# Cutting the token parts of a feed-forward stage as 384, 512, 512, 384 instead of 512, 512, 512, 256, with the weights split in the first two parts

## The chip, the core and the metric

The kernel runs on one core of one Trainium2 chip. The metric is the device time of one execution in microseconds (us); lower is better. The engines named below are PE (TensorE), DVE (VectorE), ACT (ScalarE), POOL (GpSimd) and SP (SyncE, which here issues the DMAs of the last stage).

## What is computed

Three layers follow each other: a sigmoid attention, a layer of eight experts of which one is taken per token, and a dense feed-forward layer with a rational activation. The change lies in the last one. For 1792 tokens of 768 values and a hidden width of 2048:

```python
h = x @ w_in
h2 = h * h
h3 = h2 * h
P = a[0] + a[1] * h + a[2] * h2 + a[3] * h3
Q = 1.0 + np.abs(b[0]) * np.abs(h) + np.abs(b[1]) * h2
g = P / (Q + 1e-06)
return (g @ w_out).astype(np.float32)
```

## The kernel before

`attention` and `experts` run first and are not touched. While they run, they also decode the weights of the last layer to single precision and leave them in DRAM (`wd`), 16 blocks of 128 hidden columns, each holding its slice of `w_in` and of `w_out`.

`ffn` (lines 849 to 1029) is the last stage. The tokens are cut into parts (`Q`, line 855): 512, 512, 512 and 256. Within a part it runs over the 16 blocks (`f`); one block of one part is called a unit here, and `i` counts the 64 units. To keep single precision, every operand is split in a high half and a low half that TensorE takes in its faster format, and every product is made of three matmuls (high by high, low by high, high by low).

A unit has these steps:

- `l1(i)`: 18 matmuls (lines 941, 942 and 945), input `xh`, `xl` by the unit's `w_in` block, into one PSUM bank `ph`. There are two such banks.
- `act1` and `act2`: the activation on the bank, five ACT instructions and eight DVE instructions (lines 953 to 976). The last two leave the halves `gh` and `gl`.
- `l2(i)`: 18 matmuls (lines 989 to 991), `gh`, `gl` by the unit's `w_out` block, added into six PSUM banks `acc` that hold the part's output. At the last block of a part these are copied out (`ot`, lines 995 and 997) and stored (line 998).

Each engine takes its instructions in program order. The loop (lines 1011 to 1029) sets that order: in turn `i` PE gets `l1(i)` and then `l2(i - 2)`, so two units of lead lie between a unit's first and second product, and the activation runs in them.

In the first part (`i < 16`) the weights come raw: `load` (line 866) fetches a block from `wd`, `split` (line 881) makes the halves of it by two ACT copies and two DVE subtractions of 128x768 (lines 888, 889), two units ahead, and `keep` (line 891) stores the halves to `ws`. In the later parts `fetch` (line 875) reads the halves back. SP issues all of these in program order.

The next part's tokens are prepared meanwhile: at `f == 2` they are loaded (`rows`, line 896), at `f` 5 to 8 DVE multiplies one chunk of 128 tokens a unit by its gate (`gate`, line 905, instruction at line 910), and at `f` 9 to 14 `xprep` (line 912) makes one of six blocks of `xh` and `xl` a unit: PE transposes (line 918) into a `ph` bank, an ACT copy (line 919), a DVE subtraction (line 920). The first part's tokens are prepared by `first_x` (line 922), after 26 matmuls on constants (line 927) that keep PE at work while the tokens are fetched.

The order of DVE's work in a turn is: the gate or the `xl` subtraction of that turn, the two subtractions of `split(i + 2)`, and the eight instructions of the activation.

Of the kernel before, what the change touches and what calls it, by code (L numbers as in the profile page):

```python
# [8 lines left out]
F32 = mybir.dt.float32  # L9
F32R = mybir.dt.float32r  # L10
# [10 lines left out]
P = 128  # L21
B, H, S, D = 4, 12, 448, 64
NT = B * S
# [4 lines left out]
KD = DM // P  # L28
# [15 lines left out]
def build(tc, qT, kT, v, emb, tau, w1, w2, w_in, w_out, pa, pb, out, dbg=None):  # L44
    nc = tc.nc
    with ExitStack() as ctx:
        ctx.enter_context(tc.manual_schedule())
        cst = ctx.enter_context(tc.tile_pool(name="cst", bufs=1))
        drm = ctx.enter_context(tc.tile_pool(name="drm", bufs=1, space=DRAM))
        st = dict(cst=cst, drm=drm, dbg=dbg, nc=nc, w1=w1, w2=w2, raw={})  # L50
        stg = ctx.enter_context(tc.tile_pool(name="stg", bufs=5))
        st["stg"] = stg
        st["wd"] = drm.tile([F2 // P, P, 2, DM], F32, name="wd")
        st["ws"] = [drm.tile([F2 // P, P, 2, DM], F32, name=f"ws{i}") for i in range(2)]
        st["rdy"] = [tc.alloc_semaphore(f"rdy{i}") for i in range(4)]
        with tc.tile_pool(name="wq", bufs=1) as wq:
            st["W"] = [[wq.tile([P, KD, 512], F32R, name=f"w{u}{x}") for x in "hl"] for u in range(2)]
            attention(tc, st, qT, kT, v, emb, tau, w_in, w_out, pa, pb)
            experts(tc, st, w1, w2, w_in, w_out)
        ffn(tc, st, out)  # L60
        if dbg is not None:
            dump(tc, st, dbg)
# [786 lines left out]
def ffn(tc, st, out):  # L849
    nc = tc.nc  # L850
    wd, yd, ident = st["wd"], st["yd"], st["ident"]
    gt = st["gr"]
    co, ab1, one = st["co"], st["ab1"], st["one"]
    NF = F2 // P
    Q = [(t, min(512, NT - t)) for t in range(0, NT, 512)]
    NQ = len(Q)
    NU = NQ * NF
    LF = 2
    with ExitStack() as ctx:
        fw = ctx.enter_context(tc.tile_pool(name="fw", bufs=2, reuse_waits="tile"))  # L860
# [3 lines left out]
        X, R, WI, WO, G, acc, KEPT = {}, {}, {}, {}, {}, {}, {}  # L864

        def load(i):
            if i < NF:
                R[i] = st["stg"].tile([P, 2, DM], F32, name="rw", tag="raw")
                nc.sync.dma_start(R[i], wd[i])

        def pair(i):
            for part, D_, n in ((0, WI, 4), (1, WO, 6)):
                D_[i] = fw.tile([P, 2, DM], F32R, name="wi" if part == 0 else "wo", bufs=n)

        def fetch(i):
            if NF <= i < NU and i not in WI:
                pair(i)
                for part, D_ in ((0, WI), (1, WO)):
                    nc.sync.dma_start(D_[i].bitcast(F32), st["ws"][part][i % NF])

        def split(i):
            if i >= NF:
                return
            raw = R.pop(i)
            pair(i)
            for part, D_ in ((0, WI), (1, WO)):
                w = KEPT[part, i] = D_[i]
                nc.scalar.copy(w[:, 0], raw[:, part])
                nc.vector.tensor_sub(w[:, 1], raw[:, part], w[:, 0])

        def keep(i):
            if 0 <= i < NF:
                for part, D_ in ((0, WI), (1, WO)):
                    nc.sync.dma_start(st["ws"][part][i], KEPT.pop((part, i)).bitcast(F32))

        def rows(q, parts):
            t0, w = Q[q]
            yq = fp.tile([P, 4, DM], F32, name="yq", bufs=1)
            src = yd[t0 : t0 + w].rearrange("(c p) d -> p c d", p=P)
            n = w // P // parts  # L900
            for c in range(0, w // P, n):
                nc.sync.dma_start(yq[:, c : c + n], src[:, c : c + n])
            X[q] = dict(y=yq, n=w, c=w // P)

        def gate(q, c):
            if c >= X[q]["c"]:
                return
            ci = Q[q][0] // P + c
            y = X[q]["y"][:, c]
# [11 lines left out]

        def first_x():
            d = X[0]
            d["h"], d["l"] = [fw.tile([P, KD, 512], F32R, name=n) for n in ("xh", "xl")]
            pts = [ppa.tile([P, 512], F32, name=f"acc{k}") for k in range(KD)]
            for _ in range(26):
                nc.tensor.matmul(pts[0], lhsT=st["ones"], rhs=st["wz"], start=True, stop=True)  # L927
            for c in range(4):
                for k in range(KD):
                    nc.tensor.transpose(pts[k][:, c * P : (c + 1) * P], d["y"][:, c, k * P : (k + 1) * P], ident)  # L930
            for k in range(KD):
                nc.scalar.copy(d["h"][:, k], pts[k])  # L932
                nc.vector.tensor_sub(d["l"][:, k], pts[k], d["h"][:, k])

        def l1(i):
            w = WI.pop(i)
# [30 lines left out]
        def act2(i, t1, q, r0):  # L967
            w = Q[i // NF][1]
            n = fp.tile([P, 512], F32, name="n")[:, :w]
            nc.vector.scalar_tensor_tensor(n, q, 1.000001, r0, op0=ALU.add, op1=ALU.mult)  # L970
            nc.vector.scalar_tensor_tensor(n, n, 2.0, r0, op0=ALU.subtract, op1=ALU.mult, reverse0=True)  # L971
            nc.vector.scalar_tensor_tensor(t1, t1, co[:, 0:1], n, op0=ALU.add, op1=ALU.mult)  # L972
            gh = fp.tile([P, 512], F32R, name="gh", bufs=3)[:, :w]
            gl = fp.tile([P, 512], F32R, name="gl", bufs=3)[:, :w]
            nc.vector.tensor_copy(gh, t1)  # L975
            nc.vector.tensor_sub(gl, t1, gh)  # L976
            G[i] = (gh, gl)

        def l2(i):
            q, f = divmod(i, NF)  # L980
            w = WO.pop(i)
            t0, m = Q[q]
            gh, gl = G.pop(i)
# [16 lines left out]
        for i in range(4):  # L1000
            load(i)
        split(0)
        split(1)
        rows(0, 4)
        keep(0)
        load(4)
        load(5)
        for c in range(4):
            gate(0, c)
        first_x()  # L1010
        for i in range(NU + LF):
            if i < NU:
                q, f = divmod(i, NF)
                if q + 1 < NQ:
                    if f == 2:
                        rows(q + 1, 1)
                    if 5 <= f < 9:
                        gate(q + 1, f - 5)
                    if 9 <= f < 9 + KD:
                        xprep(q + 1, f - 9)  # L1020
                ph = l1(i)
                split(i + 2)
                keep(i + 1)
                load(i + 6)
                fetch(i + 2)
                fetch(i + 3)
                act2(i, *act1(ph, X[i // NF]["n"]))
            if i >= LF:
                l2(i - LF)
# [44 lines left out]
```

## Time and profile before

| what | value |
|---|---|
| median of 3 runs | 1059.98 us (1059.35 to 1060.36) |
| the profiled execution | 1062.73 us, span 1061.0 us from its first to its last instruction |
| PE busy | 1015.2 us, 96% of the span |
| PE weight loads busy | 798.5 us, 75% |
| DVE busy | 720.4 us, 68% |
| ACT busy | 516.4 us, 49% |
| mean granted TensorE clock | 0.983 of full speed |
| last stage | first product at 587.43 us, last matmul at 1056.72 us |

The shares are means over the whole program. The last stage takes some 470 us of it, and within it the first part has other work on DVE, ACT and the DMA queues than the rest, so the shares have to be read part by part.

### The profile page before, as it was taken

To read this page: it belongs to the slowest core of one execution; us is meant where nothing else is said; L and a number is where in the kernel's file an instruction comes from. 1 tells how busy PE (TensorE), PEld (TensorE's weight loads), DVE (VectorE), ACT (ScalarE), POOL (GpSimd) and SP (SyncE) were. 2 spreads that over 40 slices of the span, in tenths; PEclk is the share of its full clock that TensorE was granted. 3 is DMA by queue.
4 is the path that set the end of the run, shared out by engine and by line. 5 is a ranking of instruction groups with operands and counts; after the bars stand their busy time and mean duration, and the time that the engine had idled before them with its cause. 6 is when DMAs were issued, how large, how long until landed. Compare 5 with 4: busy or idle time off the path is not lost. (4 is left out here: it accounts for less than half of the span.)

```text
span 1061.0 us, 14341 instructions
## 1 busy us (share of the span) xinstructions
PE 1015.2 (96%) x5227; PEld 798.5 (75%) x5228; DVE 720.4 (68%) x1036; ACT 516.4 (49%) x871; POOL 133.0 (13%) x141
## 2 busy tenths in 40 slices
PE   8999999487999999999996999999999999999998
PEld 3444444276898989889884788888888888888998
DVE  2567667579901988083955899976677666666686
ACT  5565656442323323233333676745555455554664
POOL 2000000024322332242433000000000000000000
PEclk9999999789999999999998999999999999999999
DMA  7999987578731887275767997586755566555892
GB/s 232 264 273 290 300 261 222 182 264 282 251 128 62 269 268 253 105 227 184 230 182 217 415 365 289 223 299 235 272 185 180 187 237 240 198 181 193 316 407 93
DMA packets 105580, 250.99 MB, mean 237 GB/s; under 512 B 11785, under 2 KB 59081, under 8 KB 105489
## 3 DMA queue, kind: packets, MB, share of 16 engines
q1 hardware_dynamic: 102416, 235.19, 65.9%
q0 software_dynamic: 3072, 14.58, 4.0%
q8 instruction: 58, 0.95, 0.4%
q14 instruction: 34, 0.27, 0.1%
HBM read 194.68 MB, written 55.06 MB: 235 GB/s over the span
## 5 line engine op out<-in xcount | busy, mean ns | idle before, releaser
L989 PE MATMUL acc<-gh,wo 128*128 128x512 f32 (+1 forms) x384 | 139.3, 363 | 0.3 <-DVE gh L975 0.3
L991 PE MATMUL acc<-gl,wo 128*128 128x512 f32 (+1 forms) x384 | 139.4, 363 | 0.0
L990 PE MATMUL acc<-gh,wo 128*128 128x512 f32 (+1 forms) x384 | 139.2, 363 | 0.0
L941 PE MATMUL ph<-xh,wi 128*128 128x512 f32 (+1 forms) x384 | 137.8, 368 | 0.1
L942 PE MATMUL ph<-xh,wi 128*128 128x512 f32 (+1 forms) x384 | 136.1, 363 | 0.0
L953 ACT COPY h<-ph 128x512 f32<-128x512 f32 (+1 forms) x64 | 34.0, 532 | 158.1 <-PE ph L945 158.1
L960 DVE SCALAR_TENSOR_TENSOR sq<-sq,ab,ab 128x512 f32<-128x512 f32 (+1 forms) x64 | 43.8, 684 | 91.8 <-ACT ab L957 91.8
L176 ACT ACTIVATE A<-sc,bias_s 128x896 f32<-128x896 f32 x96 | 88.7, 1008 | 27.2 <-PE sc L173 25.3
L616 DVE CAST w0h<-raw 128x1536 fp32r<-128x1536 f32 x14 | 12.8, 957 | 115.9 <-ACTq L741 115.0
L945 PE MATMUL ph<-xl,wi 128*128 128x512 f32 (+1 forms) x384 | 87.2, 363 | 0.0
L941 PEld LDWEIGHTS ph<-xh,wi 128*128 128x128 f32 x384 | 72.5, 189 | 12.1 <-ACT xh L932 1.3
L989 PEld LDWEIGHTS acc<-gh,wo 128*128 128x128 f32 x384 | 72.5, 189 | 11.7 <-DVE gh L975 0.6
L991 PEld LDWEIGHTS acc<-gl,wo 128*128 128x128 f32 x384 | 72.5, 189 | 11.5 <-DVE gl L976 0.2
L990 PEld LDWEIGHTS acc<-gh,wo 128*128 128x128 f32 x384 | 72.5, 189 | 11.2
L942 PEld LDWEIGHTS ph<-xh,wi 128*128 128x128 f32 x384 | 72.5, 189 | 10.8
L173 PE MATMUL sc<-qr,kr 64*128 64x448 f32 x384 | 78.7, 549 | 0.0
L185 PE MATMUL po<-A,vt 128*64 128x448 f32 x384 | 77.5, 545 | 0.0
L945 PEld LDWEIGHTS ph<-xl,wi 128*128 128x128 f32 x384 | 66.7, 189 | 11.2
L728 PE MATMUL py<-w2h,h 128*128 128x384 f32 x256 | 62.8, 344 | 4.9 <-DVEq L625 4.0
L728 PE MATMUL ph<-w0h,x 128*128 128x512 f32 x192 | 59.6, 410 | 8.3 <-DVEq L625 3.7
L738 ACT ACTIVATE hs<-ph 128x512 f32<-128x512 f32 x38 | 22.7, 598 | 81.8 <-PE ph L728 81.8
L728 PE MATMUL py<-w3h,h 128*128 128x384 f32 x256 | 61.3, 339 | 0.0
(199 smaller groups left out, 1975.7 us busy)
## 6 DMA issues: line engine op xcount, KB each, us to landing
raw<-in_w_dram SPq DMA_DIRECT2D x64, 768.0 KB, 6.8
wi<-ws SPq DMA_DIRECT2D x48, 768.0 KB, 4.3
wo<-ws SPq DMA_DIRECT2D x48, 768.0 KB, 4.4
raw<-in_w_in_dram SPq DMA_DIRECT2D x16, 768.0 KB, 6.9
raw<-in_w_out_dram SPq DMA_DIRECT2D x16, 768.0 KB, 7.2
wd<-dec SPq DMA_DIRECT2D x32, 384.0 KB, 3.5
rw<-wd SPq DMA_DIRECT2D x16, 768.0 KB, 9.8
ws<-wi SPq DMA_DIRECT2D x16, 768.0 KB, 6.4
```

The source lines that it names most:

```text
L173: nc.tensor.matmul(sc[:, r, :S], lhsT=d["k"][rs, c * P : (c + 1) * P], rhs=d["q"][rs], start=True, stop=True)
L176: nc.scalar.activation(A[:, c], sc[:, :, :S], AF.Sigmoid, bias=st["bias_s"], scale=0.125)
L185: nc.tensor.matmul(po[r * D : r * D + D, :S], lhsT=vt[:, c, 2 * (p % 3) + r], rhs=A[:, c, r], start=(c == 0), stop=(c == 3),)
L728: m = nc.tensor.matmul(d[u], lhsT=a, rhs=w, start=(g == 0 and n == 0), stop=(g == 1 and n == len(work) - 1))
L941: nc.tensor.matmul(ph, lhsT=w[:, 0, js], rhs=xh[:, k], start=(k == 0), stop=False)
L942: nc.tensor.matmul(ph, lhsT=w[:, 1, js], rhs=xh[:, k], start=False, stop=False)
L945: nc.tensor.matmul(ph, lhsT=w[:, 0, js], rhs=xl[:, k], start=False, stop=(k == KD - 1))
L953: nc.scalar.copy(h, ph)
L960: nc.vector.scalar_tensor_tensor(sq, sq, ab1, ab, op0=ALU.mult, op1=ALU.add)
L989: nc.tensor.matmul(a, lhsT=w[:, 0, js], rhs=gh, start=(f == 0), stop=False)
L990: nc.tensor.matmul(a, lhsT=w[:, 1, js], rhs=gh, start=False, stop=False)
L991: nc.tensor.matmul(a, lhsT=w[:, 0, js], rhs=gl, start=False, stop=(f == NF - 1))
```

## The change

The cut becomes 384, 512, 512 and 384. The weights are loaded raw and split in the first two parts (`i < 32`); only the second part stores the halves, and the third and fourth read them back. `first_x` handles three chunks of 128 tokens instead of four.

```diff
-    Q = [(t, min(512, NT - t)) for t in range(0, NT, 512)]
+    Q = [(0, 384), (384, 512), (896, 512), (1408, 384)]
...
         def load(i):
-            if i < NF:
+            if i < 2 * NF:
                 R[i] = st["stg"].tile([P, 2, DM], F32, name="rw", tag="raw")
-                nc.sync.dma_start(R[i], wd[i])
+                nc.sync.dma_start(R[i], wd[i % NF])
...
         def fetch(i):
-            if NF <= i < NU and i not in WI:
+            if 2 * NF <= i < NU and i not in WI:
...
         def split(i):
-            if i >= NF:
+            if i >= 2 * NF:
                 return
...
         def keep(i):
-            if 0 <= i < NF:
+            if NF <= i < 2 * NF:
                 for part, D_ in ((0, WI), (1, WO)):
-                    nc.sync.dma_start(st["ws"][part][i], KEPT.pop((part, i)).bitcast(F32))
+                    nc.sync.dma_start(st["ws"][part][i % NF], KEPT.pop((part, i)).bitcast(F32))
...
-            d["h"], d["l"] = [fw.tile([P, KD, 512], F32R, name=n) for n in ("xh", "xl")]
+            d["h"], d["l"] = [fw.tile([P, KD, 512], F32R, name=n)[:, :, : d["n"]] for n in ("xh", "xl")]
...
-            for c in range(4):
+            for c in range(d["c"]):
...
-                nc.scalar.copy(d["h"][:, k], pts[k])
-                nc.vector.tensor_sub(d["l"][:, k], pts[k], d["h"][:, k])
+                nc.scalar.copy(d["h"][:, k], pts[k][:, : d["n"]])
+                nc.vector.tensor_sub(d["l"][:, k], pts[k][:, : d["n"]], d["h"][:, k])
...
-        rows(0, 4)
+        rows(0, 3)
```

How the built program changes is shown at two places. The first is DVE in one unit of the first part (the seventh, `i` = 6), with one gate for the next part; each row is an instruction with its output, its inputs and the output's partitions and elements. Before:

```order
L910 TENSOR_SCALAR yq<-yq,gr 128x768
L889 TENSOR_TENSOR wi<-rw,wi 128x768
L889 TENSOR_TENSOR wo<-rw,wo 128x768
L960 SCALAR_TENSOR_TENSOR sq<-sq,ab_200,ab 128x512
L963 TENSOR_TENSOR t_8950<-t_8950,h 128x512
L964 SCALAR_TENSOR_TENSOR t_8950<-t_8950,co,h 128x512
L970 SCALAR_TENSOR_TENSOR n<-sq,ab 128x512
L971 SCALAR_TENSOR_TENSOR n<-n,ab 128x512
L972 SCALAR_TENSOR_TENSOR t_8950<-t_8950,co,n 128x512
L975 CAST gh<-t_8950 128x512
L976 TENSOR_TENSOR gl<-t_8950,gh 128x512
```

The same unit on DVE in the changed program:

```order
L910 TENSOR_SCALAR yq<-yq,gr 128x768
L889 TENSOR_TENSOR wi<-rw,wi 128x768
L889 TENSOR_TENSOR wo<-rw,wo 128x768
L960 SCALAR_TENSOR_TENSOR sq<-sq,ab_200,ab 128x384
L963 TENSOR_TENSOR t_8926<-t_8926,h 128x384
L964 SCALAR_TENSOR_TENSOR t_8926<-t_8926,co,h 128x384
L970 SCALAR_TENSOR_TENSOR n<-sq,ab 128x384
L971 SCALAR_TENSOR_TENSOR n<-n,ab 128x384
L972 SCALAR_TENSOR_TENSOR t_8926<-t_8926,co,n 128x384
L975 CAST gh<-t_8926 128x384
L976 TENSOR_TENSOR gl<-t_8926,gh 128x384
```

The eleven instructions are the same and in the same order; the eight of the activation are shorter by a quarter of their columns, the gate and the two of the split keep their size.

The second place is PE in the first part, where the first two blocks of the next part's input are transposed (`i` = 9 and `i` = 10), each ahead of that unit's first product; the names in brackets are the engines or DMA queues whose semaphores the instruction waits for. Before:

```order
L918 MATMUL ph_9123<-ident_157,yq_8633 128x128 [waits DMAHW0_49,Activation_49]
L918 MATMUL ph_9123<-ident_157,yq_8633 128x128
L918 MATMUL ph_9123<-ident_157,yq_8633 128x128 [waits DVE_49] x2
L941 MATMUL ph_9130<-xh_8463,wi_9003 128x512 [waits Activation_49]
...
L918 MATMUL ph_9198<-ident_157,yq_8633 128x128 [waits DVE_49]
L918 MATMUL ph_9198<-ident_157,yq_8633 128x128 x3
L941 MATMUL ph_9205<-xh_8463,wi_9072 128x512 [waits Activation_49]
```

The same place on PE in the changed program:

```order
L918 MATMUL ph_9095<-ident_157,yq_8619 128x128 [waits DMAHW1_49,Activation_49]
L918 MATMUL ph_9095<-ident_157,yq_8619 128x128
L918 MATMUL ph_9095<-ident_157,yq_8619 128x128 [waits DVE_49] x2
L941 MATMUL ph_9102<-xh_8459,wi_8979 128x384 [waits Activation_49]
...
L918 MATMUL ph_9168<-ident_157,yq_8619 128x128 [waits Activation_49]
L918 MATMUL ph_9168<-ident_157,yq_8619 128x128 x3
L941 MATMUL ph_9175<-xh_8459,wi_9046 128x384 [waits DVE_49]
```

In both programs the third and fourth transpose of `i` = 9 wait for DVE, which has to have scaled the third and fourth chunk. From `i` = 10 on the two `ph` banks are handed out the other way round: the transposes now wait for ACT's copy of the unit before, and the first matmul of `l1` waits for DVE's `xl` subtraction of the unit before, where previously the transposes waited for it.

## Rows read from the trace of the kernel before

**Rows 1.** Stretch: us, busy PE, PEld, DVE, ACT, POOL (instructions), PE clock, DMA share, GB/s.
```profile
256.90:260.20 3.30, 3.30 (x9) 2.55 (x8) 3.30 (x4) 0.00 (x0) 3.00 (x2) 0.50 0.84 296
587.00:718.00 131.00, 130.87 (x589) 107.61 (x588) 118.55 (x172) 88.23 (x138) 0.00 (x0) 1.00 0.82 313
```

**Rows 2.** Chain that ended last: start us, us, what; ends of six first products.
```profile
615.12 1.36 PE ph L945 x6
623.28 1.36 PE ph L945 x6
...
656.39 1.36 PE ph L945 x6
...
665.04 1.36 PE ph L945 x6
...
1040.29 0.72 PE ph L945 x6
1044.61 0.72 PE ph L945 x6
```

**Rows 3.** Timeline, PE in the experts: start us, us, instruction, idle before and releaser.
```profile
250.11 0.34 PE L728 MATMUL py<-w3h,h 128*128 128x384 f32 x1
...
251.32 0.34 PE L728 MATMUL py<-w3l,h 128*128 128x384 f32 x1
255.39 0.98 PE L728 MATMUL ph<-w0h,x 128*128 128x512 f32 x3 [3.72 <-DVEq L625]
```

**Rows 4.** Timeline, start of the last stage, all engines.
```profile
584.52 2.78 PE L930 MATMUL acc<-ident,yq 128*128 128x128 f32 x24
...
586.79 3.04 ACT L932 CAST xh<-acc 128x512 fp32r<-128x512 f32 x6 [7.13 <-PE acc L930]
...
587.43 0.50 PE L941 MATMUL ph<-xh,wi 128*128 128x512 f32 x1
...
592.03 0.59 ACT L953 COPY h<-ph 128x512 f32<-128x512 f32 x1 [0.75 <-PE ph L945]
...
593.92 0.75 DVE L960 SCALAR_TENSOR_TENSOR sq<-sq,ab,ab 128x512 f32<-128x512 f32 x1 [1.11 <-ACT ab L957]
```

**Rows 5.** Timeline, first part, around the preparation of the second part's input.
```profile
652.56 0.61 DVE L910 TENSOR_SCALAR yq<-yq,gr 128x768 f32<-128x768 f32 x1
...
653.04 0.60 PE L918 MATMUL ph<-ident,yq 128*128 128x128 f32 x4
...
660.48 0.68 DVE L920 TENSOR_TENSOR xl<-ph,xh 128x512 fp32r<-128x512 f32 x1
...
668.32 0.68 DVE L920 TENSOR_TENSOR xl<-ph,xh 128x512 fp32r<-128x512 f32 x1
```

**Rows 6.** Groups by shape, last stage: instruction xcount | busy, mean ns | idle before.
```profile
L960 DVE SCALAR_TENSOR_TENSOR sq<-sq,ab,ab 128x512 f32<-128x512 f32 x48 | 36.0, 750 | 80.9 <-ACT ab L957 80.9
L970 DVE SCALAR_TENSOR_TENSOR n<-sq,ab 128x512 f32<-128x512 f32 x48 | 33.2, 692 | 1.7
...
L975 DVE CAST gh<-t 128x512 fp32r<-128x512 f32 x48 | 20.5, 427 | 3.5
...
L960 DVE SCALAR_TENSOR_TENSOR sq<-sq,ab,ab 128x256 f32<-128x256 f32 x16 | 7.8, 485 | 10.9 <-ACT ab L957 10.9
...
L970 DVE SCALAR_TENSOR_TENSOR n<-sq,ab 128x256 f32<-128x256 f32 x16 | 6.8, 425 | 1.3
...
L975 DVE CAST gh<-t 128x256 fp32r<-128x256 f32 x16 | 4.7, 295 | 1.7
```

**Rows 7.** Timeline, PE at the end: the last unit's second product begins.
```profile
1053.68 0.28 PE L991 MATMUL acc<-gl,wo 128*128 128x256 f32 x1
1054.31 0.39 PE L989 MATMUL acc<-gh,wo 128*128 128x256 f32 x1 [0.35 <-DVE gh L975]
```

**Rows 8.** DMA issues of the last stage: xcount, KB each, median us to landing.
```profile
out_dram<-ot SPq DMA_DIRECT2D x18, 256.0 KB, 2.9
...
out_dram<-ot SPq DMA_DIRECT2D x6, 128.0 KB, 1.8
```

## The prediction

> **What bounds the kernel now.** I read the busy times by stretch first. In the first part of the last stage PE is busy 130.87 of 131 us, and DVE 118.55 of the same 131 [rows 1]: two engines are full there, and only one can give. The chain of waits that ended last then shows PE alone from the first product to the end, in even steps. The ends of the first products of two neighbouring units lie 8.16 us apart with 512 tokens (615.12 to 623.28), 8.65 where a unit also prepares the next part's input (656.39 to 665.04), and 4.32 with 256 tokens (1040.29 to 1044.61) [rows 2]. A unit has 36 matmuls, so one costs 0.2267 us at 512 columns and 0.1200 at 256. With 384 columns the experts show it: seven steps from 250.11 to 251.32, 0.173 each [rows 3]. The three lie on one line, so a unit of 384 tokens costs PE 36 x 0.1733 = 6.24 us.
>
> The third thing to see is how little room DVE has in the first part. The fourth transpose for the second part's input needs the chunk that DVE scales last. DVE ends that at 652.56 + 0.61 = 653.17; the four transposes start at 653.04 [rows 5], 0.11 apart (24 of them take 2.78 us with the last one's own 0.27 [rows 4]), so the fourth starts near 653.37. The chunk is ready 0.2 us before PE asks.
>
> **The change, part by part.**
>
> *Matmuls.* Before, 16 x (3 x 8.16 + 4.32) = 460.8 us; after, 16 x (2 x 6.24 + 2 x 8.16) = 460.8. Nothing, as the cost is a line in the columns and the count of matmuls is the same.
>
> *Head.* `first_x` transposes 18 blocks instead of 24, at 0.11 each: 6 fewer save 0.65. The first ACT copy is of 384 columns, 0.1 shorter. The first product starts 0.75 earlier, at 586.68. Bounds: nothing (if the third chunk came late) to -0.75. The dropped stores can only make that chunk come sooner, so I take -0.75.
>
> *Transposes in later parts.* 24 + 24 + 18 instead of 24 + 24 + 12; four cost PE 8.65 - 8.16 = 0.49 [rows 2], so six more cost 0.7.
>
> *End.* Before, PE waits for the last unit's `gh`: the step from 1053.68 to 1054.31 is 0.63 instead of 0.12 [rows 7]. With 384 tokens the two second products that run meanwhile last 6.24 instead of 4.32 us, 1.92 more, and the activation in front of `gh` grows by about 1.3 (1.0 on DVE and 0.3 on ACT, as below). The wait goes: -0.5. The last copy and store are larger: a store of 128 KB lands in 1.8 us and one of 256 KB in 2.9 [rows 8], so 192 KB costs between 0 and 1.1 more; half of it, 0.55, less what other traffic put on the larger ones, and 0.2 for copy and last matmul: I take +0.5.
>
> *Stores and loads.* The first part drops 32 stores, the second has 16 raw loads and 32 stores where it had 32 fetches. That is the traffic that the first part has now, 313 GB/s with PE full [rows 1], at the same unit length of 8.16 us, and a raw block is asked for four units ahead. Nothing; the cover is those four units.
>
> *Splits in the second part.* Two ACT copies and two DVE subtractions a unit. A unit of 512 tokens with split is what the first part runs now without holding PE. Nothing, as long as DVE enters the second part no later than it enters the first now.
>
> *The first part on DVE.* This is the term that decides. PE's unit shrinks from 8.16 to 6.24, by 1.92. DVE's unit keeps the split and the gates and shrinks only in its eight activation instructions, each by half of what lies between 512 and 256 columns: 0.265/2 for L960 (the same for two others), 0.267/2 for L970 (and three others), 0.132/2 for L975 [rows 6]: (3 x 0.265 + 4 x 0.267 + 0.132)/2 = 1.00. Follow both from the first product to that fourth transpose:
>
> - PE needs 653.04 - 587.43 = 65.61 us now [rows 4, 5]: nine first and seven second products, 0.96 less each. After: 65.61 - 15.36 = 50.25, and the fourth transpose follows 0.33 later, at 50.6.
> - DVE ends the chunk at 653.17 - 587.43 = 65.74 now. Eight activations lie ahead of it, 8 x 1.00 less. Its first starts 593.92 - 587.43 = 6.49 after the first product [rows 4], and that lead-in shrinks by about 1.3: 1.0 in the first product (18 matmuls of 0.0533 less), and 0.3 in ACT's three instructions from 592.03 to 593.92 [rows 4], if these shrink in the proportion of DVE's (1.00 of 5.45). So 56.4.
>
> The chunk comes 56.4 - 50.6 = **5.8 us** too late. PE loses that, part of it already at `gh` and `gl` of the units before. Then DVE keeps the pace: its step with an `xl` subtraction is 668.32 - 660.48 = 7.84 [rows 5], less 1.00 is 6.84, against 8.65 - 1.92 = 6.73 on PE; five such steps cost 5 x 0.11 = 0.55. The `ph` banks that change places do not alter this: each wait on DVE there is for the same subtraction. At the turn to the second part ACT's output copies stand behind an activation that is late; between 0 and 0.8, and I take 0.3 (the late DVE has two units of 8.16 us to recover in). Together 6.65.
>
> *Sum.* -0.75 + 0.7 - 0.5 + 0.5 + 6.65 = **+6.6 us**. The profiled execution, 1062.73 us, would become 1069.3. It stands 2.75 above the median of the runs, 1059.98; the difference carries over, so the forecast is **1066.6 us**. From the second part on PE never has to wait: a unit with split gains some 0.8 us on DVE.
>
> **Rivals.**
>
> *PE's clock falls in the wait.* In the experts PE stands still for 3.72 us before 255.39 [rows 3], and soon after the granted clock is 0.50, 1.2 GHz, for the stretch 256.90 to 260.20 [rows 1]. If some 4 us of the 5.8 come in one piece at the transposes, the same can follow. Half speed for 3.3 us costs 1.65, but the 0.55 + 0.3 of later waits are then filled: +0.8, 1067.4 us. The Trainium skill (TensorE: Matmul & The Clock Gate, Why this matters for your kernels) warns of idle gaps between bursts of matmuls for this reason; rows 3 and 1 agree with it. Against it: earlier waits may take more of the 5.8 and leave a shorter gap.
>
> *DVE's cost goes with the columns.* If all eight instructions shrank by a quarter (1.36 a unit: a quarter of 3 x 0.750 + 4 x 0.692 + 0.427), the chunk would be late by 5.8 - 8 x 0.36 = 2.9 and the steps after it shorter than PE's: +2.9 with the other terms' -0.05, 1062.8 us. Rows 6 speak against it: half the columns take 65% of the time. The Trainium skill (VectorE: DVE Perf Modes, the section on the TRN2 errata) says that such instructions pay a fixed time each and advises 512 elements and more, which is against a part of 384; for an addition of 384 elements its formula gives 557 ns as an estimate, and half way between rows 6 lies 558.
>
> *No wait at all (not slower).* The two units of lead hold the lag, and only the other terms show: -0.05, 1059.9 us. That needs DVE to gain 15.1 us up to that chunk, nearly as PE does, instead of 9.3; the point is a lag under some 2 us, which is what can be measured. For it would speak idle time on DVE in the first part that could shrink; but 118.55 of 131 are busy there, and the chunk is ready only 0.2 us early now.
>
> *The second part's traffic.* Outputs of the first part, a token load, raw loads and stores meet; were a raw block late by more than those four units (over 30 us), PE would lose several us more, 1070 or above. The 313 GB/s of the first part, with PE full, speak against it.
>
> **How the numbers follow.** Forecast 0.54, clock 0.25, columns 0.09, no wait 0.06, traffic 0.04, other 0.02. An error of 0.1 us a unit in DVE's step is 1.3 us over the first part, and the store and turn add 0.5 each way. The range 1063.5 to 1069.5 takes in forecast and clock with these, and about a third of the columns case. A measurement tells 0.2%, about 2.1 us, from no change: slower 0.92, same 0.06, faster 0.02.
>
> **What would show it.** In the first part PE should have a gap of about 4 us at L918 (waiting for L910 on DVE) near 639 to 643 us, short waits at L989 and L991 for L975 and L976 in the units ahead of it and of 0.1 to 0.2 at L941 after it, and DVE should be busy without a break from some 590 to 700. The first product should start near 586.7, the second, third and fourth part should run without waits, and the wait at 1054.31 should be gone. A DVE step of 6.2 us in units without a gate, or a first part of PE without gaps, would prove me wrong.

## The result, and the profile after

| | before | after |
|---|---|---|
| median of 6 runs each | 1060.69 us (1059.35 to 1061.92) | 1068.78 us (1067.14 to 1069.98) |
| ratio | | 1.0075 [1.0062, 1.0088] |
| the profiled execution, its span | 1062.73, 1061.0 us | 1069.98, 1068.2 us |
| first product starts | 587.43 | 585.77 |
| start of the first product to start of the last matmul | 469.29 | 478.34 |
| start of the last matmul to the end of the span | 4.28 | 4.09 |

The change is slower, as forecast: by 8.1 us where the sum had 6.6, at a time inside the range. The two profiled executions differ by 7.25 us only, because the code ahead of the last stage, which is the same in both, happened to end 1.02 us earlier in the second (the warm-up matmuls start at 575.78 instead of 576.80). From those matmuls to the end the last stage takes 484.20 us before and 492.42 after, 8.22 more. Between the first product and the last matmul it is 9.05 us more; the stretch ahead of the first product gives back 0.64 and the end 0.19. One run of the old cut below, of twelve, took 1151.22 us at a mean granted clock of 0.842 and is left out of its figures.

Windows of the changed kernel show in which part: the first part, the stretch right behind its gap, and the three other parts (columns: us from and to, us, busy PE, PEld, DVE, ACT, POOL with instructions, PE clock, DMA share, GB/s).

```profile
587.00:696.00 109.00, 104.51 (x580) 101.10 (x580) 102.80 (x172) 79.35 (x139) 0.00 (x0) 0.97 0.43 152
...
642.70:648.60 5.90, 5.90 (x19) 5.90 (x20) 5.47 (x10) 3.09 (x5) 0.00 (x0) 0.50 0.35 133
...
696.00:830.00 134.00, 134.00 (x611) 111.89 (x611) 117.52 (x170) 89.41 (x138) 0.00 (x0) 1.00 0.78 296
830.00:957.00 127.00, 127.00 (x571) 105.19 (x570) 87.82 (x134) 65.70 (x105) 0.00 (x0) 1.00 0.59 211
957.00:1064.00 107.00, 107.00 (x607) 105.32 (x606) 74.52 (x134) 56.08 (x105) 0.00 (x0) 1.00 0.57 201
```

In the first part PE was full before, 130.87 of 131 us [rows 1]; now 4.5 us are missing, and for 5.9 us the clock stands at half, 1.2 GHz. From 696 on PE is full at the full clock, in the second part too, which now has the splits and the stores.

The list of waits of PE and its weight loads in the last stage (us in total, times, longest):

```profile
PE ph L918 <- DVE yq L910: 4.1, 1, 4.1
...
PEld acc L991 <- DVE gl L976: 1.4, 5, 0.4
PEld acc L989 <- DVE gh L975: 0.9, 2, 0.5
```

One wait stands out: the transpose for the gate of the last chunk. The timeline of PE and DVE shows it, with DVE's steps around it (start us, us, instruction, idle before and releaser).

```profile
585.77 0.44 PE L941 MATMUL ph<-xh,wi 128*128 128x384 f32 x1
...
597.37 0.61 DVE L960 SCALAR_TENSOR_TENSOR sq<-sq,ab,ab 128x384 f32<-128x384 f32 x1
...
603.68 0.61 DVE L960 SCALAR_TENSOR_TENSOR sq<-sq,ab,ab 128x384 f32<-128x384 f32 x1
...
609.98 0.61 DVE L960 SCALAR_TENSOR_TENSOR sq<-sq,ab,ab 128x384 f32<-128x384 f32 x1
...
616.42 0.61 DVE L960 SCALAR_TENSOR_TENSOR sq<-sq,ab,ab 128x384 f32<-128x384 f32 x1
...
634.59 0.56 DVE L976 TENSOR_TENSOR gl<-t,gh 128x384 fp32r<-128x384 f32 x1
...
635.20 0.45 PE L991 MATMUL acc<-gl,wo 128*128 128x384 f32 x1
...
637.33 0.61 DVE L960 SCALAR_TENSOR_TENSOR sq<-sq,ab,ab 128x384 f32<-128x384 f32 x1
...
638.09 0.49 PE L918 MATMUL ph<-ident,yq 128*128 128x128 f32 x3
...
642.02 0.61 DVE L910 TENSOR_SCALAR yq<-yq,gr 128x768 f32<-128x768 f32 x1
...
642.69 0.47 PE L918 MATMUL ph<-ident,yq 128*128 128x128 f32 x1 [4.11 <-DVE yq L910]
...
644.29 0.61 DVE L960 SCALAR_TENSOR_TENSOR sq<-sq,ab,ab 128x384 f32<-128x384 f32 x1
...
649.20 0.69 DVE L920 TENSOR_TENSOR xl<-ph,xh 128x512 fp32r<-128x512 f32 x1
...
651.79 0.60 PE L918 MATMUL ph<-ident,yq 128*128 128x128 f32 x4
...
656.11 0.69 DVE L920 TENSOR_TENSOR xl<-ph,xh 128x512 fp32r<-128x512 f32 x1
...
1064.11 0.34 PE L991 MATMUL acc<-gl,wo 128*128 128x384 f32 x1
```

Read DVE's steps off the starts of L960: 603.68 - 597.37 = 6.31 us for an early unit without a gate, 616.42 - 609.98 = 6.44 for the last one before the gates, 644.29 - 637.33 = 6.96 with a gate, and 656.11 - 649.20 = 6.91 with an `xl` subtraction. PE's unit costs 6.24 [rows 3], and 6.73 with transposes by the forecast. DVE is slower in every kind of unit, and PE's second products come to wait for `gh` and `gl`.

That PE then stands still for 4.11 us in one piece follows from where the gate stands in DVE's queue. The second product ahead of the transposes needs `gl` of the unit `i` = 6, which DVE ends at 634.59 + 0.56 = 635.15. The transposes need the gate behind the activation of `i` = 7, and that gate ends at 642.02 + 0.61 = 642.63. That is 7.48 us of DVE's work, beside which PE has only the rest of that second product, 638.09 - 635.20 = 2.89, and three transposes.

The chain of waits that ended last says the same in another way (start us, us, what). It was PE alone in this stretch; now it passes over to DVE at 601.96 and comes back only with the gate.

```profile
600.90 1.05 PE ph L945 x6
601.96 0.94 DVE wi L889
...
642.02 0.62 DVE yq L910
642.69 0.47 PE ph L918
```

For 41 us PE is not in the chain: it runs through DVE, with ACT's L961 between DVE's steps. On the page of the profile, PE's share of that chain is 42% of the span and DVE's 3%.

### The profile page after: what moved, and what is told of

Read it like the earlier page. It is cut to its first block, busy times and chain, and to the rows that moved or that the text cites. A ratio compares the mean times of both kernels' runs of the same rounds, so it can differ in the third digit from the quotient of the medians.

```text
span 1068.2 us, 14353 instructions
## 1 busy us (share of the span) xinstructions
PE 1022.4 (96%) x5228; PEld 825.3 (77%) x5228; DVE 747.8 (70%) x1068; ACT 539.2 (50%) x903; POOL 131.4 (12%) x141
## 5 line engine op out<-in xcount | busy, mean ns | idle before, releaser
L941 PE MATMUL ph<-xh,wi 128*128 128x512 f32 (+1 forms) x384 | 142.2, 370 | 0.0
L942 PE MATMUL ph<-xh,wi 128*128 128x512 f32 (+1 forms) x384 | 140.3, 365 | 0.0
L953 ACT COPY h<-ph 128x384 f32<-128x384 f32 (+1 forms) x64 | 34.2, 534 | 138.0 <-PE ph L945 138.0
L960 DVE SCALAR_TENSOR_TENSOR sq<-sq,ab,ab 128x384 f32<-128x384 f32 (+1 forms) x64 | 43.7, 683 | 72.0 <-ACT ab L957 71.7
L941 PEld LDWEIGHTS ph<-xh,wi 128*128 128x128 f32 x384 | 73.0, 190 | 8.0 <-ACT xh L932 0.3
L945 PEld LDWEIGHTS ph<-xl,wi 128*128 128x128 f32 x384 | 70.7, 190 | 7.5
```

What stands on the lines that cost most here:

```text
L941: nc.tensor.matmul(ph, lhsT=w[:, 0, js], rhs=xh[:, k], start=(k == 0), stop=False)
L942: nc.tensor.matmul(ph, lhsT=w[:, 1, js], rhs=xh[:, k], start=False, stop=False)
L945: nc.tensor.matmul(ph, lhsT=w[:, 0, js], rhs=xl[:, k], start=False, stop=(k == KD - 1))
L953: nc.scalar.copy(h, ph)
L960: nc.vector.scalar_tensor_tensor(sq, sq, ab1, ab, op0=ALU.mult, op1=ALU.add)
```

## The experiments

Times are medians; a ratio is to the kernel before on the same chip, whose median there was 1062.0. "Length" is from the start of the first product to the start of the last matmul in the profile: 469.29 us before, 478.34 in the change. Where an edit adds lines, the rows have the line numbers of the edited kernel (L921 for L918, for example). The theory is that DVE's rate in the first part is the loss: the split and the gates don't shrink with the part, PE's work does.

### The change with the old cut

Edit on the changed kernel; the splits in two parts and the stores in the second stay:

```diff
-    Q = [(0, 384), (384, 512), (896, 512), (1408, 384)]
+    Q = [(0, 512), (512, 512), (1024, 512), (1536, 256)]
...
-        rows(0, 3)
+        rows(0, 4)
```

> The old cut 512, 512, 512, 256, with the other half of the change: weights split in the first two parts, halves stored in the second alone. Theory 'rate': DVE's unit of 512 tokens with split (7.4 us) is under PE's 8.16, so nothing waits: same as before within 0.15%, 1059.5 to 1062, first product to last matmul 469 to 470 us. Rival 'second part' (the loss comes from splits, raw loads and stores there): most of the 8 us, 1065 to 1069.

Measured: 1061.38 us, ratio 0.9991 [0.9977, 1.0005], length 469.28. Between first product and end the list has one wait of PE, of 0.3 us at the end, the old one of [rows 7]. The window over its second part, which splits and stores:

```profile
718.00:850.00 132.00, 132.00 (x596) 109.24 (x595) 115.22 (x165) 87.18 (x134) 0.00 (x0) 1.00 0.77 292
```

PE is full at 292 GB/s. The second part's traffic and its splits cost nothing, and dropping the first part's stores gains nothing. That rival falls.

### The new cut without the second split

The kernel before with the new `Q` and three chunks first (`first_x` has the change's widths, which are left out here); the weights are split, and stored, in the first part alone:

```diff
-    Q = [(t, min(512, NT - t)) for t in range(0, NT, 512)]
+    Q = [(0, 384), (384, 512), (896, 512), (1408, 384)]
...
-        rows(0, 4)
+        rows(0, 3)
```

> The new cut 384, 512, 512, 384 alone: weights split and their halves stored in the first part, read back in the other three. Theory 'rate': DVE's queue in the first part is that of the change, so the loss is the same: 1067.5 to 1070, a gap of about 4 us on PE at L918 waiting for L910, and the clock at half after it. Rival 'second part': 1060 to 1062.

Measured: 1068.9 us, ratio 1.0065 [1.0046, 1.0083], length 478.32, which is the change's to 0.02 us. The list of waits has the same row:

```profile
PE ph L918 <- DVE yq L910: 4.1, 1, 4.1
```

With the one before, this settles that the loss comes from the cut, and that the rest of the change is worth nothing in either direction.

### A first part of 256 tokens

```diff
-    Q = [(0, 384), (384, 512), (896, 512), (1408, 384)]
+    Q = [(0, 256), (256, 512), (768, 512), (1280, 512)]
...
-        rows(0, 3)
+        rows(0, 2)
```

> The changed kernel with the cut 256, 512, 512, 512: the suspected cost enlarged. PE's unit in the first part falls to 4.32 us, DVE's to some 5.4 (5.9 with a gate, 5.85 with an xl subtraction, against 4.81 on PE). Theory 'rate': PE is held from the first unit on, by 21 to 24 us over the first part: first product to last matmul 489 to 493 us, time 1080 to 1084. Rival 'one wait' (a fixed wait for the gate, not a rate): the loss stays near 8 us or grows only by the 0.64 us of the head, 1067 to 1071.

Measured: 1084.3 us, ratio 1.0205 [1.0189, 1.0221], length 491.68. DVE's timeline gives its step there:

```profile
595.21 0.48 DVE L960 SCALAR_TENSOR_TENSOR sq<-sq,ab,ab 128x256 f32<-128x256 f32 x1
...
600.56 0.48 DVE L960 SCALAR_TENSOR_TENSOR sq<-sq,ab,ab 128x256 f32<-128x256 f32 x1
```

5.35 us against PE's 4.32 [rows 2]. A quarter of the tokens fewer cost 9 us of length; another 128 tokens fewer cost 13.3 more. The length lies in the range expected, the time 0.3 above it. The loss grows as the two steps move apart, but not in proportion:

```profile
PE acc L989 <- DVE gh L975: 5.2, 7, 1.2
PE ph L918 <- DVE yq L910: 4.0, 1, 4.0
```

The wait for the last gate is as long as in the change, 4.0 and 4.1. What grew are the waits for `gh`, and waits of PE for ACT came in, 4.8 us in all. Read so, the difference of the steps decides how long PE waits at its second products, and the place of the gate sets the one long wait. Whether gates a unit earlier would spare that wait, or only move it to later units, was not tried.

### The small parts last

Again on the change: the same sizes, but the two parts of 384 behind the two that split.

```diff
-    Q = [(0, 384), (384, 512), (896, 512), (1408, 384)]
+    Q = [(0, 512), (512, 512), (1024, 384), (1408, 384)]
...
-        rows(0, 3)
+        rows(0, 4)
```

> The changed kernel with the cut 512, 512, 384, 384: two parts of 384 as in the change, but none of them with a split. Theory 'rate': DVE's unit of 512 with split fits (7.4 against 8.16), its unit of 384 without split is 4.7 against 6.24, so nothing waits, and the wait at the end goes too: first product to last matmul 468.3 to 469.3 us, time 1059.5 to 1061.5. Rival 'shape' (parts of 384 cost by themselves): some 4 to 8 us more than before.

Measured: 1061.2 us, ratio 0.9992 [0.9981, 1.0002], length 468.38. Between first product and last matmul the list has no wait of PE, and none of over 0.4 us of its weight loads. Its first part and its first part of 384:

```profile
587.00:718.00 131.00, 131.00 (x590) 108.00 (x589) 123.20 (x178) 92.55 (x143) 0.00 (x0) 1.00 0.40 138
...
843.00:944.00 101.00, 101.00 (x577) 98.96 (x576) 74.39 (x134) 56.65 (x105) 0.00 (x0) 1.00 0.76 268
```

So a part of 384 as such is no loss. Where its unit has no split, DVE is busy 74.39 of 101 us and keeps up. The length is 0.9 us less than before, with the wait at the end gone, but the interval of the times holds 1: it can't be told from the kernel before.

### PE kept busy in the gap

To see what the clock costs, 16 matmuls on constants go ahead of the transposes that wait, into the same bank, which the first transpose overwrites:

```diff
             pt = pph.tile([P, 512], F32, name="ph")[:, : d["n"]]
+            if q == 1 and k == 0:
+                for _ in range(16):
+                    nc.tensor.matmul(pt, lhsT=st["ones"], rhs=st["wz"], start=True, stop=True)
```

> The changed kernel with 16 matmuls on constants (3.6 us at full clock) into the bank of the first transposes, ahead of them, where PE stands still for 4.1 us; their result is overwritten by the transposes. Theory: they fit into the gap, the clock does not fall, and what the half clock cost is regained: 5.9 us at half speed after the gap are 2.9 us of PE's work, of which DVE's pace after the gap would have taken 0.6 to 1.0 anyway, so 1.9 to 2.3 us less than the change: 1066.3 to 1067.3. Rival (the half clock cost nothing, since DVE sets the pace in the whole first part): same as the change, 1068.5 to 1069.5.

Measured: 1067.79 us, ratio 1.0054 [1.0036, 1.0072], length 477.10. PE's timeline at the place, then the window behind it:

```profile
637.25 3.63 PE L919 MATMUL ph<-wz,ones 128*128 128x512 bf16 x15
...
641.86 0.33 PE L921 MATMUL ph<-ident,yq 128*128 128x128 f32 x1 [0.66 <-DVE yq L910]
...
648.28 0.60 PE L921 MATMUL ph<-ident,yq 128*128 128x128 f32 x4
```

```profile
643.00:649.00 6.00, 5.88 (x36) 5.60 (x34) 5.45 (x11) 4.83 (x9) 0.00 (x0) 1.00 0.35 132
```

The clock stays at 1.00, and the fourth transpose comes 56.91 us after the first product (641.86 - 584.95), as late as in the change (642.69 - 585.77 = 56.92). (One of the sixteen matmuls has no record.) The length falls by 1.24 us. That is what the clock cost, net: less than expected, more than nothing. The medians alone would not tell it, as this ratio's interval overlaps that of the change; the lengths do, which agree to 0.02 us where two kernels have the same order of work (the change and the new cut without the second split).

From the fourth transpose to the next unit's transposes PE took 651.79 - 642.69 = 9.10 us in the change and 648.28 - 641.86 = 6.42 here, so the low clock lost 2.68. But DVE sets the pace right behind the gap, and PE at full speed waits there: in this run's list of waits its weight loads wait five times for the `xl` subtraction, 1.2 us in all, and once at the turn to the second part, 0.2, waits that the change's list doesn't have.

```profile
PEld ph L944 <- DVE xl L923: 1.2, 5, 0.5
```

PE's slowness and DVE's lie side by side, and 1.4 of the 2.68 are covered.

### The gates on ACT

```diff
-            nc.vector.tensor_scalar(y, y, gt[:, ci : ci + 1], None, op0=ALU.mult)
+            if q == 1:
+                nc.scalar.activation(y, y, AF.Identity, scale=gt[:, ci : ci + 1])
+            else:
+                nc.vector.tensor_scalar(y, y, gt[:, ci : ci + 1], None, op0=ALU.mult)
```

> The changed kernel with the four gates of the second part's tokens on ACT instead of DVE (ACT is busy 79 of 109 us there). Theory 'rate' (DVE's unit is too long in all of the first part, the gate is only where PE meets it first): DVE is relieved of 4 x 0.53 = 2.1 us, the rest of the lag shows at the next places where PE needs DVE or ACT behind DVE (transposes and first products of units 9 and 10), in shorter pieces, so the clock need not fall (1.2 us more): first product to last matmul 474.5 to 476.5 us against 478.3, time 1064.5 to 1066.5. Rival 'the gate's place' (with the gate out of DVE's queue nothing else is late): 469 to 470.5 us, time 1059.5 to 1061.5.

Measured: 1066.78 us, ratio 1.0040 [1.0026, 1.0053], length 474.79. Two waits of PE and two of DVE's steps, then the window behind the waits:

```profile
617.01 0.61 DVE L963 SCALAR_TENSOR_TENSOR sq<-sq,ab,ab 128x384 f32<-128x384 f32 x1
...
623.45 0.61 DVE L963 SCALAR_TENSOR_TENSOR sq<-sq,ab,ab 128x384 f32<-128x384 f32 x1
...
639.03 0.33 PE L921 MATMUL ph<-ident,yq 128*128 128x128 f32 x1 [0.92 <-ACT yq L911]
640.86 0.44 PE L944 MATMUL ph<-xh,wi 128*128 128x384 f32 x1 [1.50 <-ACT h L956]
```

```profile
642.20:645.50 3.30, 3.30 (x12) 3.30 (x12) 3.12 (x6) 2.32 (x5) 0.00 (x0) 0.50 0.51 138
```

3.55 us come back, not the nine; the length is as expected, the time 0.3 over its range. The wait for the gate shrinks but does not go: the gate now stands on ACT behind activations that wait for DVE, and the second wait is for ACT's copy, which stands behind the gate. Without gates DVE's unit is still 623.45 - 617.01 = 6.44 us against 6.24. And the clock, which was not expected to fall, does so again, after two short waits. As the edit loads ACT, it does not price the gate's place by itself.

### One subtraction of the split on POOL

POOL is idle in the first part (0.00 in every window above). It takes the subtraction of the `w_out` block while `i < 16`:

```diff
-                nc.vector.tensor_sub(w[:, 1], raw[:, part], w[:, 0])
+                eng = nc.gpsimd if part and i < NF else nc.vector
+                eng.tensor_sub(w[:, 1], raw[:, part], w[:, 0])
```

> The changed kernel, with one of the two weight subtractions of a unit of the first part (the low half of wo) on POOL instead of DVE. Theory 'rate' (in the first part DVE's unit of split and activation is longer than PE's 6.24 us, and PE waits for it): DVE's unit falls by 0.87 us to some 5.5, under PE's; no wait at the transposes, no fall of the clock, first product to last matmul some 468.5 to 469.5 us instead of 478.3, time 1059.5 to 1061. Rival 'shape' (parts of 384 cost PE more by themselves) or 'second part' (its splits and stores cost): stays at 1067 to 1069. Against 'rate' only in size: should POOL's subtraction take over some 5 us, or slow DVE while it runs, the wait comes back.

Measured: 1078.09 us, ratio 1.0147 [1.0127, 1.0168], length 486.12: worse than the change by 7.8, where it was expected to gain some nine. What came is the reservation at the end of the expectation. DVE's step without a gate, with POOL beside it:

```profile
612.55 0.61 DVE L961 SCALAR_TENSOR_TENSOR sq<-sq,ab,ab 128x384 f32<-128x384 f32 x1
...
615.91 2.01 POOL L890 TENSOR_TENSOR wo<-rw,wo 128x768 fp32r<-128x768 f32 x1 [4.96 <-ACT wo L888]
...
616.32 1.82 DVE L976 CAST gh<-t 128x384 fp32r<-128x384 f32 x1
...
619.59 0.61 DVE L961 SCALAR_TENSOR_TENSOR sq<-sq,ab,ab 128x384 f32<-128x384 f32 x1
```

DVE's step is 7.04 us, against 6.44 in the same unit of the change, though 0.87 of work was taken from it. The cast to `gh` lasts 1.82 us instead of 0.36 and ends 0.22 after POOL does (618.14 and 617.92). It was held up while POOL worked.

### POOL again, with the cast replaced

To see whether only the cast is held up, the edits of the last two runs together, and in the first part `gh` from a second L972 instead of the cast:

```diff
-            nc.vector.scalar_tensor_tensor(t1, t1, co[:, 0:1], n, op0=ALU.add, op1=ALU.mult)
...
-            nc.vector.tensor_copy(gh, t1)
+            if i < NF + 1:
+                nc.vector.scalar_tensor_tensor(gh, t1, co[:, 0:1], n, op0=ALU.add, op1=ALU.mult)
+                nc.vector.scalar_tensor_tensor(t1, t1, co[:, 0:1], n, op0=ALU.add, op1=ALU.mult)
+            else:
+                nc.vector.scalar_tensor_tensor(t1, t1, co[:, 0:1], n, op0=ALU.add, op1=ALU.mult)
+                nc.vector.tensor_copy(gh, t1)
```

> The changed kernel with a first part in which DVE gets less to do and nothing of it meets POOL: the low half of wo on POOL, the gates of the second part's tokens on ACT, and the high half gh written by the same arithmetic instruction as t (0.62 us) instead of by the cast (0.36 us alone, 1.82 us while POOL subtracts, as the first run of this study showed). DVE's unit: 6.45 - 0.87 + 0.26 = 5.84 us, 6.44 with an xl subtraction, under PE's 6.24 and 6.73. Theory 'rate', with the cast as the reason why the subtraction on POOL made it worse: no waits in the first part, first product to last matmul 468.5 to 469.5 us, time 1059 to 1061, at or just under the kernel before. Rival (POOL slows all of DVE's instructions): waits as before, over 1066.

Measured: 1079.08 us, ratio 1.0157 [1.0137, 1.0176], length 487.30. The expectation fell. DVE and POOL in two units:

```profile
608.55 0.62 DVE L979 SCALAR_TENSOR_TENSOR gh<-t,co,n 128x384 fp32r<-128x384 f32 x1
...
608.86 2.01 POOL L890 TENSOR_TENSOR wo<-rw,wo 128x768 fp32r<-128x768 f32 x1 [5.15 <-ACT wo L888]
...
609.20 2.09 DVE L980 SCALAR_TENSOR_TENSOR t<-t,co,n 128x384 f32<-128x384 f32 x1
...
624.17 1.91 POOL L890 TENSOR_TENSOR wo<-rw,wo 128x768 fp32r<-128x768 f32 x1 [6.05 <-ACT wo L888]
...
624.48 2.01 DVE L984 TENSOR_TENSOR gl<-t,gh 128x384 fp32r<-128x384 f32 x1
```

It is not the cast. The instruction that DVE had begun before POOL, at 608.55, kept its 0.62 us. The next, of the very same kind and size, lasts 2.09 and ends 0.42 after POOL; in the other unit it is the subtraction to `gl` that lasts 2.01. In both runs the one instruction that DVE begins while POOL subtracts lasts until POOL is done, whether a cast, a scalar_tensor_tensor or a subtraction.

Whether ACT could take DVE's cast to `gh`, or a part of the split, was not tried and stays open.

## Why the prediction was right, and where its sizes were off

| term of the sum | forecast | measured | from |
|---|---|---|---|
| head | -0.75 | -0.64 | first warm-up matmul (576.80, 575.78) to first product: 10.63 before, 9.99 after |
| lateness of the last chunk | +5.8 | +6.3 | 642.69 - 585.77 = 56.92 against 50.6 |
| later waits for DVE and ACT | +0.85 | some +1.3 | length with the clock kept up, less the other terms; 1.2 + 0.2 in its list of waits |
| clock in the gap | left to a rival, +0.8 | +1.24 | length with and without matmuls in the gap |
| transposes, wait at the end | +0.7 - 0.5 | not separable | the wait is gone from the list |
| end | +0.5 | -0.19 | 4.28 before, 4.09 after |
| last stage | +6.6 | +8.22 | 484.20 to 492.42 |

**The deciding term held.** The method was to follow both engines from the first product to the one transpose where they meet. The chunk was to be done 56.4 us after the first product; it was at 642.63 - 585.77 = 56.86. Half the column span as a measure for 384 columns held as well, in the groups by shape (instruction xcount, busy, mean ns):

```profile
L960 DVE SCALAR_TENSOR_TENSOR sq<-sq,ab,ab 128x384 f32<-128x384 f32 x32 | 19.7, 615 | 25.5 <-ACT ab L957 25.5
...
L970 DVE SCALAR_TENSOR_TENSOR n<-sq,ab 128x384 f32<-128x384 f32 x32 | 17.9, 559 | 2.7
...
L975 DVE CAST gh<-t 128x384 fp32r<-128x384 f32 x32 | 11.5, 361 | 2.7
```

The middles of [rows 6] are 618, 558 and 361 ns. The rival in which the cost goes with the columns is out; "no wait at all" falls by the wait itself. DVE's steps came out 6.96 with a gate and 6.91 with an `xl`; before they were 652.56 - 644.64 = 7.92 (starts of L910) and 7.84 [rows 5], which less the forecast's 1.00 gives 6.92 and 6.84. Without a gate they were 6.31 to 6.44, where 6.2 was named as the sign of being wrong. The extra 0.5 us of lateness is 0.05 us a unit over nine units, within the error that the range allowed. The lateness showed as forecast: 4.1 us in one piece at L918, and 2.3 before it in the waits for `gl` and `gh` (1.4 and 0.9 in the list).

**The step that was mis-sized is the clock.** The forecast took it as a rival of 0.25, with a fall of 3.3 us as in the experts; the fall came and held for 5.9, and its net price was 1.24 instead of 0.8. What spoke against it, that earlier waits might shorten the gap, did not happen: the gap was to be "some 4 us" in the text of that rival, and a gap of 3.72 had done it before [rows 3]. With the clock in the sum, the forecast would have been 1067.4, and with its measured price 1067.8. The Trainium skill (TensorE: Matmul & The Clock Gate, Why this matters for your kernels) warns of gaps between bursts of matmuls; the change's 4.11 us agrees.

**Later waits.** Five `xl` steps were to cost 0.55, the turn to the second part 0.3. The run with the clock kept up shows 1.2 for the five and 0.2 for the turn. The 0.11 a unit was the difference of two numbers of nearly the same size, and both were a little off: DVE's step is 6.91 instead of 6.84, and PE's is 6.70 instead of 6.73 (behind the slow stretch its transposes stand in the chain at 658.64, 665.35 and 672.04), so 0.21, or 1.05 for five. In the change itself these waits don't appear, since the slow PE covers them. This the prediction had said of its rival, but "0.1 to 0.2 at L941" as a sign to look for was wrong with the clock down.

**The end.** The stores of 192 KB land sooner than the half-way price between 128 and 256 KB says: this is their row among the DMA issues (KB each, median us to landing).

```profile
out_dram<-ot SPq DMA_DIRECT2D x12, 192.0 KB, 2.0
```

That is 0.2 more than at 128 KB [rows 8], not 0.55, and the tail as a whole became no longer. The row has the stores of the first part too.

**Luck.** The terms that were too small (lateness, later waits, clock, and 0.1 at the head) add up to some 2.3 us, and the end was 0.7 too large, so that the sum is off by 1.6 only. The time is off by 2.2: its other 0.7 or so is the median of the kernel before, 1060.69 over six runs where the forecast had 1059.98 over three.

**What cost nothing did cost nothing:** the matmuls (PE full from 696 to the end), the second part's splits and traffic (shown by the old cut with both), and the dropped stores (shown by the new cut with them).

## What to carry to other kernels

Before cutting work into other parts, list what each engine does once per unit whatever the part's size; here the split of the weights and the gates. Compare the engines' steps in the part where that fixed work lies, not the mean over the program: the engine with the fixed work speeds up less than the other when the part shrinks (DVE from 7.92 to 6.96 us, PE from 8.16 to 6.24), and the small parts belong where there is none of it. Look also at where in the engines' queues two of them meet: work that one engine asks for out of its usual place can cost one long wait. Such a wait on TensorE was dearer here than its own length, as the clock fell with it, though not by the full amount, since the other engine set the pace afterwards.

## What was not expected of the hardware

- POOL was no free help for a full DVE: a subtraction of 128x768 took 2.0 us there against 0.95 on DVE (0.87 from start to start), and one DVE instruction begun meanwhile was held up each time: 1.82 us instead of 0.36, 2.09 instead of 0.62, 2.01 instead of 0.56, each ending 0.2 to 0.4 us after POOL. The Trainium skill (SBUF — State Buffer, SBUF: two separate sides) has this as a lock on a pair of ports that DVE and POOL share, taken by whichever starts first for its whole instruction, against DVE instructions with two SBUF inputs or in a 2-port mode. The rows agree, down to the instruction that began first and kept its time: by that rule DVE stands still for most of POOL's 2.0 us to save 0.87, and both runs with POOL lost.
- The clock fell after two waits of 0.9 and 1.5 us with only one transpose between them (the gates on ACT), not only after one of 4.1 us; it then stood at 1.2 GHz for some 3.3 us there, and for 5.9 us after the long one.
